# A new order of steps on every engine, and of the loads, in a fused attention and feed-forward kernel

## Chip, cores, metric

One core of one Trainium2 chip. The metric is device microseconds (us) of that core for one execution; lower is better. The rounds of experiments ran on different chips, but each round, and so each ratio, on one chip. A profile covers about 2 us less than an execution's time, since it starts with the first instruction and ends with the last.

## The reference

```python
def _attn_ref(q, k, v):                       # B, H, S, D = 8, 8, 576, 64
    chunk = 64
    ...
    scores = (1/sqrt(D)) * q_c @ k_c.T        # within each chunk of 64 tokens
    attn = softmax(scores)
    out = attn @ v_c

def _moe_ref(x, w1, w2, w3, w_out):           # x: 4608 x 512, d_ff 1024
    a = x @ w1
    b = x @ w2
    h = a * b @ w3
    return h @ w_out
# x of the second part is the first part's output, heads side by side; float32 in and out
```

## The kernel before

The kernel is written as small steps, and a string gives the order in which they are emitted. Every instruction goes through a helper, `inorder`, that holds it to the order of emission, so the string fixes the order on each engine, the order of the loads and which waits exist. The 18 blocks of 256 tokens are numbered 0 to 17.

```python
ORDER = """
R0 R1 v0 q1 i0 k1 v1 i1 i2 q2 k2 v2 i3 q3 k3 v3 q4 k4 v4 o h0 h1 D0.0.16.64 K0 T0.0 K1 T0.1 q5 k5 v5
S0 T1.0 E0 P0 D0.1.4.512 T1.1 q6 k6 v6 N0.0 S1 D1.0.5.512 X0.0 N0.1 X0.1 A0.0 E1 B0.0 C0.0 P1 M0.0
...
"""
    for step in ORDER.split():
        do[step[0]](*(int(n) for n in step[1:].split(".") if n))
```

| letters | engine | what |
|---|---|---|
| q k v i o h | DMA, issued by GpSimd | loads; `i` brings a quarter of w1 and w2 |
| T, G | VectorE, DMA | transpose of q or k to qkT; for blocks 8 and up, moves between partitions to qkm |
| S, E, P | TensorE, ScalarE, TensorE | scores, exp, attention times v |
| N, X, H | VectorE, VectorE, DMA | normalise, transpose to xt (to xm from block 8 on, then moves xm to xt) |
| A, B | TensorE | one group of x @ w1 and x @ w2, in the two halves of one PSUM tile |
| C, M | ScalarE, VectorE | copy of A's half to a_sb; product of a_sb and B's half |
| V W Z | VectorE, TensorE, ScalarE | w3 @ w_out, once |
| O, Y, Q | TensorE, ScalarE, DMA | output matmul, copy to o_sb, store |
| D | TensorE | dummy matmuls on zeros |

```python
    ps = ctx.enter_context(tc.tile_pool(name="ps", bufs=4, space=bass.MemoryType.PSUM))
    def psum(name):
        return ps.tile([P, 2, 512], f32, tag="p", name=name)     # two halves of 512
    ...
    def do_AB(p, j, f, which):                                   # which: 0 is A, 1 is B
        ...
                mm(ps_t[p, j][:, which, i * n:(i + 1) * n],
                   lhsT=(w1, w2)[which][:, ki, f * P:(f + 1) * P], rhs=rhs[:, ki],
                   start=(ki == 0), stop=(ki == KO - 1))
    def do_C(p, j):
        a_t[p, j] = msb.tile([P, 512], f32, tag="a_sb", bufs=3, name="a_sb")
        inorder(nc.scalar.copy(a_t[p, j][:], ps_t[p, j][:, 0, :]))
    def do_M(p, j):
        ...
        inorder(nc.vector.tensor_mul(o, view(a_t.pop((p, j))[:]), view(ps_t.pop((p, j))[:, 1, :])))
```

The softmax here doesn't subtract the row's maximum and nothing guards it: scores larger than these inputs give would overflow.

## Time and profile before

| | before |
|---|---|
| time, median of 4 executions beside the new kernel | 245.07 us (244.9 to 246.0) |
| TensorE busy in the profile | 226.6 us, 93% of the span |
| VectorE, ScalarE busy | 63%, 35% |

TensorE is the bound, so a wait of TensorE is what an order can win or lose. The waits of TensorE by releaser, kernel before (columns: engine, what it wrote and line, then what ended the wait; us in total, times, longest):

```profile
PE z_ps L92 <- DVE qkT L188: 8.1, 2, 7.3
...
PE s_ps L92 <- DMA qkm<-qkT: 1.0, 1, 1.0
PE s_ps L92 <- issue: 0.8, 2, 0.5
PE ab_ps L92 <- DVE xt L263: 0.6, 2, 0.3
```

The first line is the start, when nothing is loaded yet. The others are what an order can still win after it: S12 waiting for moves, holes inside S3 and S7 for which the profile knows no releaser ("issue"), and two waits for xt.

### The profile page before, as it was taken

To read this page: it belongs to the slowest core of one execution; us is meant where nothing else is said; L and a number is where in the kernel's file an instruction comes from. 1 tells how busy PE (TensorE), PEld (TensorE's weight loads), DVE (VectorE), ACT (ScalarE), POOL (GpSimd) and SP (SyncE) were. 2 spreads that over 40 slices of the span, in tenths; PEclk is the share of its full clock that TensorE was granted. 3 is DMA by queue.
4 is the path that set the end of the run, shared out by engine and by line. 5 is a ranking of instruction groups with operands and counts; after the bars stand their busy time and mean duration, and the time that the engine had idled before them with its cause. 6 is when DMAs were issued, how large, how long until landed. Compare 5 with 4: busy or idle time off the path is not lost.

```text
span 244.5 us, 6344 instructions
## 1 busy us (share of the span) xinstructions
PE 226.6 (93%) x2731; PEld 120.8 (49%) x2753; DVE 154.2 (63%) x232; ACT 85.2 (35%) x116; POOL 82.9 (34%) x110
## 2 busy tenths in 40 slices
PE   1279999999999999999998999999999999999994
PEld 1238777874445444444444444444444444444443
DVE  1675899698799588999997789918530232143000
ACT  2411423423233344425234335253231433332322
POOL 8847875556994346763740000000000000000000
PEclk9999999999999999999999999999999999999999
DMA  7999999999999999999999913735502200400244
GB/s 178 181 183 179 185 168 203 197 192 168 166 174 217 223 222 262 180 214 197 200 210 247 294 42 89 173 78 208 149 0 88 86 0 0 173 1 1 86 172 172
DMA packets 93595, 37.63 MB, mean 154 GB/s; under 512 B 75008, under 2 KB 86528, under 8 KB 93568
## 3 DMA queue, kind: packets, MB, share of 16 engines
q0 software_dynamic: 82592, 18.88, 83.1%
q1 hardware_dynamic: 9936, 17.83, 24.1%
q10 hardware_dynamic: 1040, 0.52, 0.8%
q8 instruction: 21, 0.34, 0.6%
q14 instruction: 6, 0.05, 0.1%
HBM read 38.80 MB, written 9.44 MB: 197 GB/s over the span
## 4 chain that ended last, share of the span: by engine, by line
PE 78%; DMA 8%; DVE 6%; SPq 3%; issue 2%; POOL 2%; ACT 1%; DVEq 0%; POOLq 0%
PE ab_ps L92 43%; PE o_ps L92 22%; PE w_ps L92 6%; DMA qkm<-qkT 5%; DMA qk<-in_k_dram 3%; PE s_ps L92 3%; SPq L180 3%; PE pv L92 2%; PE z_ps L92 2%; DVE qkT L188 2%; DVE xt L263 1%; DVE xn L251 1%; DVE ab L332 1%; POOL vbuf L95 1%; ACT a_sb L317 1%
## 5 line engine op out<-in xcount | busy, mean ns | idle before, releaser
L92 PE MATMUL ab_ps<-xt,w 128*128 128x512 bf16 (+1 forms) x681 | 126.8, 342 | 1.1 <-DVE xt L263 0.6
L92 PEld LDWEIGHTS <-w 128*128 128x128 bf16 x704 | 67.4, 98 | 55.2 <-DVE xt L263 1.2
L332 DVE TENSOR_TENSOR ab<-a_sb,ab_ps 128x512 bf16<-128x512 f32 x71 | 47.9, 676 | 45.0 <-ACT a_sb L317 44.9
L317 ACT COPY a_sb<-ab_ps 128x512 f32<-128x512 f32 x71 | 41.6, 586 | 81.0 <-PE ab_ps L92 79.1
L92 PE MATMUL o_ps<-w3o,ab 128*128 128x512 bf16 (+1 forms) x285 | 63.3, 373 | 0.6
L188 DVE STREAM_TRANSPOSE qkT<-qk 128x1024 bf16<-128x1024 bf16 x36 | 45.1, 1289 | 9.2 <-ACT qk L139 5.5
L92 PEld LDWEIGHTS <-ab 128*128 128x128 bf16 x296 | 28.5, 98 | 32.3
L95 POOL DMA_DIRECT2D vbuf<-in_v_dram x40 | 33.9, 856 | 20.9 <-DMA qk<-in_q_dram 6.4
L362 ACT COPY o_sb<-o_ps 128x1024 f32<-128x1024 f32 x17 | 17.2, 1012 | 44.8 <-PE o_ps L92 41.3
L251 DVE TENSOR_TENSOR xn<-pv,rc 128x512 bf16<-128x512 f32 x36 | 24.9, 691 | 1.2
L95 POOL DMA_DIRECT2D qk<-in_k_dram x23 | 18.0, 784 | 9.1 <-DMA vbuf<-in_v_dram 6.2
L95 POOL DMA_DIRECT2D qk<-in_q_dram x23 | 18.2, 793 | 6.9 <-DMA qk<-in_k_dram 1.5
L221 ACT ACTIVATE e<-s_ps 128x1024 bf16<-128x1024 f32 x16 | 15.9, 1026 | 3.4 <-PE s_ps L92 3.3
L92 PE MATMUL w_ps<-wo,w3T 128*128 128x512 bf16 x62 | 13.9, 379 | 0.1
L271 DVE STREAM_TRANSPOSE xm<-xn 128x512 bf16<-128x512 bf16 x20 | 13.6, 697 | 0.2
L248 DVE RECIPROCAL rc<-pv 128x8 f32<-128x8 f32 x36 | 6.9, 191 | 10.5 <-PE pv L92 10.5
L95 POOL DMA_DIRECT2D w<-in_moe_w_dram x16 | 11.1, 697 | 4.5 <-DMA wo<-in_moe_w_out_dram 1.5
L92 PEld LDWEIGHTS <-e 64*32 64x32 bf16 (+1 forms) x832 | 7.9, 97 | 7.9 <-issue 6.1
L263 DVE STREAM_TRANSPOSE xt<-xn 128x512 bf16<-128x512 bf16 x16 | 11.4, 711 | 0.5
L92 PEld LDWEIGHTS <-qkT 32*64 32x64 bf16 x512 | 5.7, 117 | 11.3 <-DVE qkT L188 9.6
L92 PE MATMUL pv<-vbuf,e 64*32 64x65 bf16 (+1 forms) x832 | 10.1, 198 | 1.1 <-ACT e L221 1.1
L355 DVE COPY o_sb<-o_ps 128x256 f32<-128x256 f32 x1 | 0.4, 425 | 16.0 <-PE o_ps L92 16.0
(23 smaller groups left out, 53.9 us busy)
## 6 DMA issues: line engine op xcount, KB each, us to landing
out_dram<-o_sb SPq DMA_DIRECT2D x17, 512.0 KB, 3.5
qkm<-qkT SPq DMA_DIRECT2D x40, 128.0 KB, 6.3
vbuf<-in_v_dram POOLq DMA_DIRECT2D x32, 128.0 KB, 8.7
w<-in_moe_w_dram POOLq DMA_DIRECT2D x16, 256.0 KB, 9.6
qk<-in_q_dram POOLq DMA_DIRECT2D x11, 256.0 KB, 7.6
qk<-in_k_dram POOLq DMA_DIRECT2D x11, 256.0 KB, 9.2
xt<-xm SPq DMA_DIRECT2D x40, 64.0 KB, 2.9
wo<-in_moe_w_out_dram POOLq DMA_DIRECT2D x4, 256.0 KB, 6.9
```

The source lines that it names most:

```text
L92: return inorder(nc.tensor.matmul(*a, **kw))
L95: return inorder(nc.gpsimd.dma_start(dst, src))
L180: inorder(nc.sync.dma_start(dst, src))
L188: inorder(nc.vector.transpose(qkT_t[g][:, :, p % 2, s, heads(h)].rearrange("p e h (y t) -> p h t e y", t=2), qk_t[p][:, s, heads(h)].rearr ...
L221: inorder(nc.scalar.activation(e_t[p][:, :, heads(hh)], s_t[p][:].rearrange("p u (h q) -> p u h q", q=CH)[:, :, heads(hh)], Exp, scale=sca ...
L248: inorder(nc.vector.reciprocal(rc[:], pv[:, :, :, D:W]))
L251: inorder(nc.vector.tensor_mul(xn_t[p][:, u], pv[:, :, :, 0:D], rc.to_broadcast([P, 2, 4, D])))
L263: inorder(nc.vector.transpose(new_xt(g)[:].rearrange("p (o t) -> p o t", o=KO)[:, :, t0:t0 + UT] .rearrange("p o (m y) -> p m o y", y=BL), ...
L271: inorder(nc.vector.transpose(xm_t[g][:, u, :, m].rearrange("p o (c y) -> p c o y", y=BL), xn_t[p][:].rearrange("p u r m d -> p (u r) m d" ...
L317: inorder(nc.scalar.copy(a_t[p, j][:], ps_t[p, j][:, 0, :]))
L332: inorder(nc.vector.tensor_mul(o, view(a_t.pop((p, j))[:]), view(ps_t.pop((p, j))[:, 1, :])))
L362: inorder(nc.scalar.copy(o_sb[:], ps_t.pop(p)[:]))
```

## The change

By its author's account, the order was searched for anew by simulated annealing, on a cost model that had been refitted to instruction fetch, to the moves between partitions and to early landings of loads. Apart from the order, and the dummies (D) that may now write other tiles, nothing changes: no computation is added or taken away. The diff, cut:

```diff
-R0 R1 v0 q1 i0 k1 v1 i1 i2 q2 k2 v2 i3 q3 k3 v3 q4 k4 v4 o h0 h1 D0.0.16.64 K0 T0.0 K1 T0.1 q5 k5 v5
-S0 T1.0 E0 P0 D0.1.4.512 T1.1 q6 k6 v6 N0.0 S1 D1.0.5.512 X0.0 N0.1 X0.1 A0.0 E1 B0.0 C0.0 P1 M0.0
-A0.1 N1.0 X1.0 B0.1 C0.1 N1.1 A0.2 X1.1 B0.2 C0.2 M0.1 A1.0 T2.0 B1.0 C1.0 M0.2 A1.1 T2.1 q7 k7 v7
...
+R0 R1 v0 q1 k1 v1 i0 i2 i1 q2 k2 i3 v2 q3 k3 v3 q4 k4 h0 o h1 v4 D0.0.0.16.64 K0 T0.0 K1 T0.1 q5 k5
+v5 D0.0.0.8.512 S0 T1.0 E0 T1.1 q6 k6 P0 v6 S1 N0.0 E1 N0.1 X0.0 X0.1 A0.0 B0.0 C0.0 P1 M0.0 A0.2
+N1.0 B0.2 N1.1 A0.1 X1.0 X1.1 C0.1 B0.1 C0.2 A1.0 T2.0 B1.0 C1.0 A1.1 M0.1 M0.2 B1.1 C1.1 T2.1 q7 k7
...
+B6.1 G5.1 C6.1 X8.0 A6.4 M6.1 P9 v15 q16 k16 C6.4 B6.4 N9.0 A6.2 M6.4 B6.2 X8.1 C6.2 N9.1 A6.5 X9.0
...
+B6.7 T12.1 O4 E11 T13.0 C6.7 M6.7 T13.1 P10 v16 q17 k17 Y4 A8.3 G6.0 N10.0 B8.3 N10.1 C8.3 A8.0 M8.3
...
+A14.5 M12.7 C12.3 A12.0 B12.3 A12.4 M12.3 B12.4 X16.1 C12.4 X17.0 C12.0 A12.6 C14.5 M12.4 H8.0 B14.5
+C12.6 B12.0 M14.5 B12.6 M12.0 Q11 A12.5 X17.1 M12.6 B12.5 H8.1 A14.7 A14.6 C14.7 C12.5 B14.6 C14.6
...
-    def do_D(which, p, n, cols):
-        d, key = (s_t, p) if which == 0 else (ps_t, (p, 0))
+    def do_D(which, p, j, n, cols):
+        d, key = ((s_t, p), (ps_t, (p, j)), (pv_t, (p, 0)))[which]
```

A step of TensorE can thus be followed by a step of another group, and C can stand ahead of its own B (`C0.1 B0.1`, `C6.4 B6.4`, `C14.5 ... B14.5`).

More of the change, by code (lines that the diff above doesn't have):

```diff
@@ L9 @@
 ORDER = """
-R0 R1 v0 q1 i0 k1 v1 i1 i2 q2 k2 v2 i3 q3 k3 v3 q4 k4 v4 o h0 h1 D0.0.16.64 K0 T0.0 K1 T0.1 q5 k5 v5
-S0 T1.0 E0 P0 D0.1.4.512 T1.1 q6 k6 v6 N0.0 S1 D1.0.5.512 X0.0 N0.1 X0.1 A0.0 E1 B0.0 C0.0 P1 M0.0
-A0.1 N1.0 X1.0 B0.1 C0.1 N1.1 A0.2 X1.1 B0.2 C0.2 M0.1 A1.0 T2.0 B1.0 C1.0 M0.2 A1.1 T2.1 q7 k7 v7
-B1.1 C1.1 M1.0 S2 M1.1 A0.3 E2 T3.0 B0.3 C0.3 P2 M0.3 A1.2 N2.0 X2.0 B1.2 C1.2 N2.1 A1.3 X2.1 B1.3
-C1.3 M1.2 A2.0 T3.1 q8 k8 v8 B2.0 C2.0 M1.3 S3 T4.0 A2.1 E3 M2.0 B2.1 T4.1 q9 k9 C2.1 P3 v9 M2.1
@@ L15 @@
-A2.2 N3.0 B2.2 C2.2 X3.0 A2.3 N3.1 B2.3 X3.1 C2.3 M2.2 S4 M2.3 A3.0 E4 B3.0 C3.0 A3.1 M3.0 B3.1 C3.1
-V0 A3.2 M3.1 B3.2 C3.2 V1 A3.3 M3.2 B3.3 C3.3 V2 W0 M3.3 V3 W1 Z0 V4 V5 W2 Z1 V6 V7 T5.0 Z2 W3 T5.1
-q10 k10 T6.0 T6.1 P4 v10 q11 k11 Z3 S5 N4.0 O0 E5 X4.0 N4.1 X4.1 T7.0 O1 T7.1 Y0 Q0 T8.0 P5 v11 q12
-k12 Y1 S6 T8.1 O2 Q1 E6 N5.0 X5.0 N5.1 X5.1 O3 T9.0 T9.1 Y2 G4.0 P6 v12 q13 k13 A4.0 N6.0 B4.0 G4.1
-Y3 X6.0 N6.1 C4.0 A4.1 X6.1 B4.1 C4.1 M4.0 Q2 S7 Q3 M4.1 A4.2 E7 T10.0 B4.2 C4.2 T10.1 P7 v13 q14
@@ L20 @@
-k14 A4.3 M4.2 B4.3 N7.0 C4.3 A4.4 X7.0 M4.3 B4.4 C4.4 N7.1 A4.5 M4.4 B4.5 C4.5 X7.1 S8 M4.5 S9 E8
-A4.6 T11.0 B4.6 E9 T11.1 P8 v14 q15 k15 C4.6 A4.7 M4.6 G5.0 B4.7 C4.7 N8.0 A6.0 M4.7 B6.0 N8.1 C6.0
-G5.1 A6.1 X8.0 B6.1 M6.0 C6.1 X8.1 P9 v15 q16 k16 A6.2 M6.1 N9.0 B6.2 C6.2 N9.1 A6.3 M6.2 B6.3 C6.3
-X9.0 A6.4 M6.3 B6.4 C6.4 X9.1 A6.5 T12.0 H4.0 B6.5 C6.5 M6.4 A6.6 M6.5 B6.6 T12.1 H4.1 C6.6 S10 S11
-M6.6 E10 A6.7 T13.0 B6.7 E11 P10 v16 q17 k17 T13.1 C6.7 O4 M6.7 G6.0 N10.0 N10.1 X10.0 G6.1 P11 v17
@@ L25 @@
-Y4 X10.1 O5 N11.0 N11.1 Q4 X11.0 X11.1 T14.0 A8.0 H5.0 Y5 B8.0 T14.1 C8.0 A8.1 M8.0 B8.1 H5.1 C8.1
-T15.0 A8.2 B8.2 M8.1 C8.2 T15.1 Q5 A8.3 B8.3 C8.3 M8.2 G7.0 S12 M8.3 S13 E12 A8.4 T16.0 B8.4 E13
-G7.1 P12 T16.1 C8.4 A8.5 B8.5 M8.4 C8.5 N12.0 A8.6 M8.5 B8.6 C8.6 N12.1 A8.7 M8.6 B8.7 C8.7 X12.0
-P13 M8.7 A10.0 X12.1 B10.0 C10.0 N13.0 A10.1 M10.0 B10.1 N13.1 C10.1 A10.2 X13.0 B10.2 M10.1 C10.2
-X13.1 S14 S15 M10.2 E14 A10.3 H6.0 T17.0 B10.3 E15 P14 T17.1 C10.3 A10.4 H6.1 M10.3 B10.4 C10.4
-N14.0 A10.5 M10.4 B10.5 G8.0 C10.5 N14.1 A10.6 M10.5 B10.6 C10.6 X14.0 P15 G8.1 X14.1 A10.7 M10.6
@@ L31 @@
-B10.7 N15.0 C10.7 O6 N15.1 M10.7 X15.0 X15.1 H7.0 S16 Y6 S17 O7 E16 E17 H7.1 P16 Y7 O8 Q6 N16.0 Q7
-N16.1 X16.0 X16.1 P17 Y8 A12.0 N17.0 Q8 B12.0 N17.1 C12.0 A12.1 X17.0 B12.1 M12.0 C12.1 X17.1 A12.2
-M12.1 H8.0 B12.2 C12.2 A12.3 M12.2 B12.3 C12.3 H8.1 A12.4 M12.3 B12.4 C12.4 A12.5 M12.4 B12.5 C12.5
-A12.6 M12.5 B12.6 C12.6 A12.7 M12.6 B12.7 C12.7 O9 M12.7 O10 Y9 Q9 A14.0 Y10 B14.0 C14.0 Q10 A14.1
-M14.0 B14.1 C14.1 A14.2 M14.1 B14.2 C14.2 A14.3 M14.2 B14.3 C14.3 A14.4 M14.3 B14.4 C14.4 A14.5
-M14.4 B14.5 C14.5 A14.6 M14.5 B14.6 C14.6 A14.7 M14.6 B14.7 C14.7 O11 M14.7 O12 Y11 Q11 A16.0 Y12
@@ L37 @@
-B16.0 C16.0 Q12 A16.1 M16.0 B16.1 C16.1 A16.2 M16.1 B16.2 C16.2 A16.3 M16.2 B16.3 C16.3 A16.4 M16.3
-B16.4 C16.4 A16.5 M16.4 B16.5 C16.5 A16.6 M16.5 B16.6 C16.6 A16.7 M16.6 B16.7 C16.7 O13 M16.7 O14
-Y13 Q13 O15 Y14 Q14 O16 Y15 Q15 Y16 Q16 O17
+R0 R1 v0 q1 k1 v1 i0 i2 i1 q2 k2 i3 v2 q3 k3 v3 q4 k4 h0 o h1 v4 D0.0.0.16.64 K0 T0.0 K1 T0.1 q5 k5
+v5 D0.0.0.8.512 S0 T1.0 E0 T1.1 q6 k6 P0 v6 S1 N0.0 E1 N0.1 X0.0 X0.1 A0.0 B0.0 C0.0 P1 M0.0 A0.2
+N1.0 B0.2 N1.1 A0.1 X1.0 X1.1 C0.1 B0.1 C0.2 A1.0 T2.0 B1.0 C1.0 A1.1 M0.1 M0.2 B1.1 C1.1 T2.1 q7 k7
@@ new lines @@
+v7 A0.3 M1.1 S2 C0.3 M1.0 B0.3 E2 M0.3 P2 A1.2 T3.0 B1.2 N2.0 A1.3 N2.1 B1.3 C1.3 X2.0 C1.2 X2.1
+T3.1 q8 k8 v8 A2.0 M1.2 C2.0 S3 T4.0 B2.0 E3 A2.1 M1.3 B2.1 M2.0 C2.1 T4.1 q9 k9 P3 v9 A2.2 M2.1
+B2.2 N3.0 A2.3 X3.0 N3.1 S4 C2.3 C2.2 X3.1 B2.3 E4 M2.2 A3.3 M2.3 B3.3 V0 A3.2 V1 B3.2 C3.2 V2 C3.3
+A3.1 W0 V3 M3.3 M3.2 A3.0 V4 B3.1 C3.0 V5 Z0 B3.0 W1 C3.1 M3.1 T5.0 W2 V6 Z1 V7 T5.1 q10 k10 W3 Z2
+M3.0 T6.0 T6.1 S5 Z3 P4 v10 q11 k11 E5 O0 N4.0 T7.0 T7.1 N4.1 O1 Y0 X4.0 Q0 T8.0 T8.1 P5 v11 q12 k12
+Y1 X4.1 O2 N5.0 Q1 T9.0 N5.1 S6 T9.1 O3 E6 X5.0 G4.0 Y2 X5.1 G4.1 P6 v12 q13 k13 A4.0 Y3 N6.0 B4.0
@@ new lines @@
+X6.0 C4.0 Q2 A4.1 N6.1 B4.1 M4.0 C4.1 X6.1 S7 M4.1 A4.2 E7 T10.0 B4.2 C4.2 T10.1 P7 v13 q14 k14 A4.3
+M4.2 N7.0 B4.3 C4.3 A4.4 M4.3 A4.5 N7.1 C4.4 B4.4 X7.0 C4.5 S8 M4.4 S9 E8 B4.5 T11.0 A4.6 E9 M4.5
+B4.6 C4.6 X7.1 P8 v14 q15 k15 M4.6 A4.7 T11.1 B4.7 C4.7 N8.0 A6.0 G5.0 B6.0 M4.7 C6.0 N8.1 A6.1 M6.0
+B6.1 G5.1 C6.1 X8.0 A6.4 M6.1 P9 v15 q16 k16 C6.4 B6.4 N9.0 A6.2 M6.4 B6.2 X8.1 C6.2 N9.1 A6.5 X9.0
+B6.5 M6.2 H4.0 A6.3 X9.1 B6.3 C6.3 C6.5 A6.6 M6.3 H4.1 B6.6 M6.5 C6.6 T12.0 A6.7 S10 M6.6 S11 Q3 E10
@@ new lines @@
+B6.7 T12.1 O4 E11 T13.0 C6.7 M6.7 T13.1 P10 v16 q17 k17 Y4 A8.3 G6.0 N10.0 B8.3 N10.1 C8.3 A8.0 M8.3
+G6.1 B8.0 T14.0 C8.0 P11 v17 A8.2 M8.0 X10.0 B8.2 C8.2 N11.0 O5 X10.1 N11.1 M8.2 X11.0 A8.1 X11.1
+H5.0 Y5 T14.1 A8.5 C8.1 A8.4 T15.0 B8.5 H5.1 C8.4 C8.5 B8.1 A8.6 M8.1 B8.4 M8.5 C8.6 S12 M8.4 S13
+E12 B8.6 T15.1 A8.7 E13 M8.6 G7.0 B8.7 C8.7 P12 M8.7 A10.3 N12.0 B10.3 Q4 C10.3 G7.1 A10.0 M10.3
+A10.1 N12.1 C10.0 B10.0 C10.1 Q5 P13 M10.0 B10.1 N13.0 A10.6 M10.1 B10.6 C10.6 N13.1 A10.2 X12.0 S14
@@ new lines @@
+M10.6 C10.2 S15 B10.2 E14 T16.0 O6 E15 M10.2 T16.1 T17.0 A10.5 T17.1 Y6 P14 B10.5 C10.5 G8.0 O7
+M10.5 N14.0 N14.1 Q6 G8.1 X12.1 X13.0 P15 Y7 A10.4 N15.0 B10.4 Q7 N15.1 C10.4 O8 X13.1 M10.4 X14.0
+X14.1 S16 Y8 S17 A10.7 E16 Q8 B10.7 H6.0 C10.7 O9 E17 M10.7 X15.0 H6.1 O10 Y9 Q9 H7.0 P16 Y10 A12.2
+N16.0 B12.2 X15.1 C12.2 O11 N16.1 H7.1 M12.2 Q10 P17 Y11 A12.7 N17.0 B12.7 X16.0 C12.7 A12.3 N17.1
+A14.5 M12.7 C12.3 A12.0 B12.3 A12.4 M12.3 B12.4 X16.1 C12.4 X17.0 C12.0 A12.6 C14.5 M12.4 H8.0 B14.5
@@ new lines @@
+C12.6 B12.0 M14.5 B12.6 M12.0 Q11 A12.5 X17.1 M12.6 B12.5 H8.1 A14.7 A14.6 C14.7 C12.5 B14.6 C14.6
+M12.5 B14.7 M14.6 A14.1 M14.7 A14.3 A16.1 C14.3 B14.1 C16.1 C14.1 B16.1 M14.1 B14.3 A16.3 M14.3
+B16.3 C16.3 A12.1 M16.3 A14.0 M16.1 B12.1 C14.0 C12.1 A16.6 M12.1 A14.4 B14.0 C14.4 A16.5 M14.0
+B14.4 C16.6 B16.6 O12 M16.6 B16.5 Y12 O13 C16.5 Q12 M16.5 M14.4 A14.2 Y13 A16.2 C14.2 Q13 B16.2
+C16.2 B14.2 A16.7 M14.2 A16.4 C16.7 B16.4 B16.7 O14 M16.7 M16.2 A16.0 B16.0 C16.0 C16.4 O15 Y14
+M16.4 M16.0 Q14 O16 Y15 Q15 Y16 Q16 O17
```

## The prediction

> **What bounds the kernel now.** I read the page first, then the windows of 10 us, then the chain, then the time line around every place where TensorE did not advance.
>
> ```profile
> PE 226.6 (93%) x2731; PEld 120.8 (49%) x2753; DVE 154.2 (63%) x232; ACT 85.2 (35%) x116; POOL 82.9 (34%) x110
> PE   1279999999999999999998999999999999999994
> DVE  1675899698799588999997789918530232143000
> DMA  7999999999999999999999913735502200400244
> ```
>
> TensorE is full from about 20 us to the end, so it is the bound; but the DMA engines are as full until 138 us (slice 23), and VectorE has slices at 9 until 150 us. Reordering changes no engine's total, so what it can win is the time in which TensorE stands or runs slowly. To size that I took the steady pace from the chain:
>
> ```profile
> 182.72 6.64 PE o_ps L92 x30
> 189.36 13.81 PE ab_ps L92 x64
> ```
>
> 64 matmuls of 512 columns take 13.81 us, 216 ns each. So an A or B step of a late group is 0.86 us, an O or W step (16 matmuls) 3.45, and an A or B step of an early group (8 matmuls of 256 columns) 0.87 by its spacing in the time line. S and P take 0.64 and 0.63 us for the first eight tiles, 0.32 and 0.38 for the other ten, and each switch from the big matmuls to the small ones costs about 0.11 more. Laid end to end, all A, B, S, P, W and O give 218.1 us, plus 26 switches x 0.11 = 2.9: 221.0. The first real matmul starts at 9.54 and the last ends at 241.2, which is 231.7. **The loss is thus about 10.7 us**, and the change can win no more than part of that. It lies here:
>
> ```profile
> 9.54 1.07 PE L92 MATMUL z_ps<-qkT 32*64 32x64 bf16 x64 [7.32 <-DVE qkT L188]
> 11.74 0.75 PE L92 MATMUL pv<-vbuf,e 64*32 64x65 bf16 x64 [1.13 <-ACT e L221]
> 12.83 1.49 PE L92 MATMUL z_ps<-zero 128*128 128x512 bf16 x3 [0.33 <-issue]
> 16.91 1.49 PE L92 MATMUL z_ps<-zero 128*128 128x512 bf16 x3 [0.22 <-issue]
> 18.19 2.28 PE L92 MATMUL z_ps<-xt,w 128*128 128x256 bf16 x16
> ```
> ```profile
> 88.26 0.31 PE L92 MATMUL s_ps<-qkT 32*64 32x64 bf16 x13 [0.50 <-issue]
> 132.00 0.93 PE L92 MATMUL s_ps<-qkm 64*64 64x64 bf16 x63 [1.03 <-DMA qkm<-qkT]
> 35.73 1.92 PE L92 MATMUL ab_ps<-xt,w 128*128 128x256 bf16 x16 [0.32 <-DVE xt L263]
> ```
>
> Some 7 us are lost before 21 us (idle, and matmuls on zeros that only keep TensorE busy). Later: two waits for xt (at 25.0 and 35.7, some 0.5 each), a hole inside S3 (0.5) and one inside S7 (0.7), and S12, which takes 1.71 us instead of 0.25, so 1.5. After 142 us nothing is lost.
>
> [...]one instruction queue moved 21 packets, 0.34 MB, 16 KB each, and the holes inside S3 and S7 are 765 weight loads apart[...].[...] moves between partitions took up to 9.7 us to land while loads ran, 2.3 at best.[...] The zeros at 12.8 to 18.2 us step by 0.42 us, twice 216 ns, and the clock record at 1.0 starts at 18.9 us[...].
>
> **The change, part by part.** It removes and adds no computation; 9 dummy matmuls of 512 columns, in two places, become 8 in one, all ahead of S0.
>
> (a) **Loads at the start.** k1 goes ahead of w1/w2 quarter 0.
>
> ```profile
> 13.72 1.31 DVE L188 STREAM_TRANSPOSE qkT<-qk 128x1024 bf16<-128x1024 bf16 x1 [2.84 <-DMA qk<-in_k_dram]
> 30.42 1.32 DVE L188 STREAM_TRANSPOSE qkT<-qk 128x1024 bf16<-128x1024 bf16 x1 [0.39 <-DMA qk<-in_q_dram]
> ```
>
> The first line is T1.1, waiting for k1. Landings of loads follow one another at 1.3 to 1.5 us for 256 KB. Two of them in front go, so k1 lands at 13.7 - 2.7 = 11.0, and T1.1 ends at 12.3 instead of 15.0. N0 and X0 for both halves took 3.2 us after it (14.93 to 18.14), so A0.0 can start near 15.8 instead of 18.1, with its weights landing at 14 to 15.4. This would be 2.3 us, or about 1 if TensorE is then still at half clock.
> But the second line says that it does not last. T3.0 waits for q3, and what is loaded up to q3 is the same set in both orders, so q3 lands at 30.4 again. After the change T3.0 stands ahead of N2 and X2 on VectorE: 30.4 + 1.3 + N2.0, N2.1, X2.0, X2.1 (2 x 0.91 + 2 x 0.71) = 34.95. Before, one M (0.7) came between, and X2.1 ended at 35.67. A2.0 waits for X2.1 in both. **So the start is worth 0.7 us, not 2.3.** From T3.0 on VectorE works without pause to X3.1 (at about 44.6 instead of 45.1), which again gives A3 some 0.7 us earlier. The hole in S3 is inside this figure.
>
> (b) **S7** keeps P6, A4.0, B4.0, A4.1, B4.1 ahead of it[...]. I expect its hole of 0.5 to 0.7 again. No gain.
>
> (c) **S12** waited for the last move of qkm, landed at 131.86.
>
> ```profile
> 122.80 9.06 DMA qkm<-qkT
> ```
>
> The transposes that feed these moves stand 0.7 us later on VectorE, but S12 now has 4.3 us more TensorE work ahead of it (114.2 instead of 109.9, counted in the two orders). Without that wait S12 would start near 130.8 before, so near 134 to 135 after: the wait goes. **-1.5 us.** A small hole at P13 (0.13) goes too: -0.1.
>
> (d) **One switch more** to small matmuls (27 instead of 26): +0.1.
>
> (e) **A8 comes early.**
>
> ```profile
> 108.75 5.65 SPq L180 DMA_DIRECT2D xt<-xm  x8
> ```
>
> Those are H4's eight moves; the last landed at 120.67, over 6 us after its issue. A8.0 ran at 123.5, without waiting. In the new order the first A8 step has 3.9 us less TensorE work ahead of it, so it is due at about 119.2, while X9.1, which feeds the last moves, has the same VectorE work ahead of it, and the moves still queue behind G5's eight. If they land at 120.5 to 121.2 TensorE waits 1.3 to 2. The author says that moves were fitted anew, so perhaps they land sooner. I put +0.9, the middle of 0 and 1.8.
>
> (f) **A and B of one tile drawn apart** (32 tiles), with C between them in 26. In the trace C starts only after B's end, though it reads A's half; dependencies seem to go by tile. C ahead of B lets M follow B at once, and in all but one of the 26 another TensorE step covers C (0.59 us). The exception, B0.1, waits for its weights anyway. Counting the four PSUM tiles round, the tightest reuses have 0.0 to 0.3 us of room: I allow +0.2 for small waits. Tail: O15, O16, O17 close it as before, no change.
>
> Sum: -0.7 - 1.5 - 0.1 + 0.1 + 0.9 + 0.2 = -1.1; 244.96 - 1.1 = 243.9. I shade to **243.7**, since an order searched for on a fitted model has more likely avoided (e) than hit it.
>
> **Rivals.** (1) *The early start survives.* If q3 lands earlier because the queue of loads packs better, the 2.3 us stay: about 241.5 to 242. For it: T1.1's 2.84 us wait is real and goes. Against: the DMA engines are at 9 in slices 1 to 22, so the stream has no slack to give. (2) *The new order loses to moves and PSUM*: A8 waits 2 us, S10 (before, its moves landed 0.6 us ahead of it) waits too, tiles turn late; 245 to 246. For it: moves of 6 to 9 us during the loads, VectorE at 9 there. Against: the search weighed it. (3) *Half clock.* The dummies now end near 5.7 us[...]; 16 matmuls of 256 columns at 0.21 instead of 0.11 cost 1.7 us. Against its mattering: q3 holds A2.0 back anyway, with room of about 1.5 us. If both bind, 244.5.
>
> **Range and chances.** 2% is 4.9 us, that is 240.06; it takes nearly half of all loss, and the start, two thirds of it, is held by the loads. Rival 1 with nothing lost in (e) gives 241.5, rival 2 up to 246. Runs of the kernel before spread over 1.1 us. So 241.7 to 245.4 at 8 in 10; faster by over 2% 0.04, slower by over 2% 0.02.
>
> **What would show it.** (a) k1 landing near 11, A0.0 near 16, and A2.0 near 35.0 with a wait for xt of over 1 us, T3.0 again waiting for q at about 30.4. If A2.0 starts before 34, the step "q3 lands at the same time" is wrong. (b) A hole of 0.5 us with releaser "issue" in S7. (c) No wait for qkm at S12. (e) A wait of TensorE for DMA xt<-xm near 119; its absence would give 0.9 us back. (f) No rows of TensorE waiting for ACT a_sb. After about 160 us no wait of TensorE above 0.3 us; one there would make the prediction wrong on the high side.

For (f), the profile before has C0.0 starting 0.03 us after B0.0's last matmul (20.48 and 20.51).

## The result

| | before | after |
|---|---|---|
| median of 4 executions | 245.07 us | 247.77 us |
| range | 244.9 to 246.0 | 247.45 to 247.97 |
| ratio, 95% interval | | 1.0101 (1.0072 to 1.0130) |

Ratios in this document are the mean time of one kernel's runs over the mean of the other's in the same rounds, so they are not quite the ratio of the medians quoted. Executions over 1.5% slower than the fastest of the same kernel are left out of the means. All outputs are right. A later repeat (e15 below) gave 1.0076. The new order is slower, by 1.9 to 2.5 us; the prediction said 1.3 faster, and its range ended at 245.4.

The page of the kernel after: busy time, and TensorE and DMA in 40 slices.

```profile
PE 228.4 (93%) x2731; PEld 121.5 (50%) x2752; DVE 152.4 (62%) x232; ACT 83.3 (34%) x116; POOL 82.9 (34%) x110
PE   7268989999999989999899999999998999999994
DMA  7999999999999999999999480554531500022044
```

The 7 in the first slice is the dummies. Before, TensorE had one slice of 8 between slice 3 and the last, at 21, which is S12. Now it has 9 there and five 8s, counted from 0: at 3, 5, 14, 19 and 30, that is at 18, 31, 86, 117 and 184 us. What stands there, the waits of TensorE, kernel after, say:

```profile
PE ab_ps L92 <- DVE xt L263: 2.5, 2, 1.9
PE ab_ps L92 <- ACT a_sb L317: 1.8, 3, 0.8
...
PE ab_ps L92 <- DMA xt<-xm: 0.8, 1, 0.8
PE s_ps L92 <- issue: 0.7, 1, 0.7
```

The wait for qkm is gone, as meant. New are three waits for ScalarE's copies, 1.8 us, and one for the moves to xt, 0.8. (Of the 2.5 us for xt, 1.9 come before A0.0, where the kernel before ran dummies and work at half clock: its zeros of 512 columns step by 0.42 us there, and matmuls of that width by 0.216 us later.) The time line of TensorE has the first of the three, kernel after:

```profile
19.46 3.29 PE L92 MATMUL ab_ps<-xt,w 128*128 128x256 bf16 x24
23.42 5.40 PE L92 MATMUL ab_ps<-xt,w 128*128 128x256 bf16 x48 [0.67 <-ACT a_sb L317]
...
35.46 1.05 PE L92 MATMUL ab_ps<-xt,w 128*128 128x256 bf16 x8 [0.56 <-DVE xt L263]
```

The second row starts with B0.1. It follows A0.1 directly, with C0.1 emitted between. ScalarE's time line shows the copy that it waited for:

```profile
22.79 1.08 ACT L317 COPY a_sb<-ab_ps 128x512 f32<-128x512 f32 x2 [3.33 <-PE ab_ps L92]
```

C0.1 starts as A0.1 ends and takes 0.59 us, and B0.1 starts at its end. C reads one half of the tile and B writes the other, yet B waits, 0.67 us. Two stretches of VectorE's time line, kernel after, show what this did to block 3:

```profile
30.64 0.69 DVE L332 TENSOR_TENSOR ab<-a_sb,ab_ps 128x512 bf16<-128x512 f32 x1 [0.75 <-ACT e L221]
31.25 1.31 DVE L188 STREAM_TRANSPOSE qkT<-qk 128x1024 bf16<-128x1024 bf16 x1
```

The second row is T3.0. It doesn't wait for q3 (landed at 30.36): it waits its turn behind M0.3, the first row. The row names an exp that ended at 30.55, but M0.3 doesn't read that. It reads the copy of A0.3, which was done at 29.45, and B0.3, whose last matmul ended at 30.53. So it waits for B0.3, that is for TensorE, which is late.

Three rows of TensorE's time line much later, kernel after: B6.4, A8.3 and B14.5.

```profile
105.82 2.53 PE L92 MATMUL ab_ps<-xt,w 128*128 128x512 bf16 x10 [0.30 <-ACT a_sb L317]
...
120.86 3.61 PE L92 MATMUL ab_ps<-xt,w 128*128 128x512 bf16 x16 [0.75 <-DMA xt<-xm]
...
189.20 5.12 PE L92 MATMUL ab_ps<-xt,w 128*128 128x512 bf16 x23 [0.79 <-ACT a_sb L317]
```

And ScalarE's row of the same place as the last, kernel after:

```profile
187.59 2.05 ACT L317 COPY a_sb<-ab_ps 128x512 f32<-128x512 f32 x4 [3.73 <-PE ab_ps L92]
```

These four copies are C12.4, C12.0, C14.5 and C12.6, in that order. Five TensorE steps stand between A14.5 and B14.5, but the copy stands third in ScalarE's queue, behind C12.4, and C12.4 is emitted behind B12.4 and waits for its end. So C14.5 ran at 188.54 to 189.15, and B14.5 after it.

Step starts (the start of a step's first weight load), in us from each span's start, show where the two kernels drift apart ("before" is the faster of its two profiles, e1; e16 and e18 are told below):

| step | before (e1) | after | e16 | e18 |
|---|---|---|---|---|
| A0.0 | 17.69 | 15.23 | 15.24 | 15.42 |
| A1.0 | 24.68 | 24.19 | 22.92 | 23.31 |
| A2.0 | 35.62 | 35.46 | 34.47 | 34.85 |
| O0 | 67.00 | 67.15 | 66.16 | 66.54 |
| S7 | 86.50 | 86.78 | 85.81 | 86.05 |
| O17 | 236.56 | 238.19 | 238.40 | 235.02 |

2.5 us are won at A0.0, and at O0 nothing is left. The rest is lost behind S7.

### The profile page after: what moved, and what is told of

Same layout as the page of the kernel before. It is cut to its first block, busy times and chain, and to the rows that moved or that the text cites. A ratio compares the mean times of both kernels' runs of the same rounds, so it can differ in the third digit from the quotient of the medians.

```text
span 245.3 us, 6362 instructions
## 1 busy us (share of the span) xinstructions
PE 228.4 (93%) x2731; PEld 121.5 (50%) x2752; DVE 152.4 (62%) x232; ACT 83.3 (34%) x116; POOL 82.9 (34%) x110
## 4 chain that ended last, share of the span: by engine, by line
PE 57%; DMA 25%; DVE 5%; POOL 5%; issue 3%; SPq 2%; ACT 1%; POOLq 0%; DVEq 0%
PE ab_ps L92 36%; PE o_ps L92 18%; DMA qk<-in_k_dram 10%; DMA qk<-in_q_dram 9%; DMA qkm<-qkT 3%; POOL vbuf L95 3%; DMA xt<-xm 3%; DVE qkT L188 2%; POOL qk L95 2%; SPq L180 2%; PE pv L92 2%; PE s_ps L92 1%; ACT a_sb L317 1%; DVE xn L251 1%; DVE ab L332 1%
## 5 line engine op out<-in xcount | busy, mean ns | idle before, releaser
L92 PE MATMUL ab_ps<-xt,w 128*128 128x512 bf16 (+1 forms) x697 | 132.0, 344 | 5.8 <-DVE xt L263 2.5
L188 DVE STREAM_TRANSPOSE qkT<-qk 128x1024 bf16<-128x1024 bf16 x36 | 45.8, 1296 | 5.9 <-ACT qk L139 5.3
L221 ACT ACTIVATE e<-s_ps 128x1024 bf16<-128x1024 f32 x17 | 17.0, 1026 | 9.2 <-PE s_ps L92 9.1
L263 DVE STREAM_TRANSPOSE xt<-xn 128x512 bf16<-128x512 bf16 x16 | 10.7, 688 | 0.1
L373 DVE STREAM_TRANSPOSE w3T<-w 128x1024 bf16<-128x1024 bf16 x8 | 9.4, 1217 | 1.1 <-DVE ab L332 0.9
L92 PEld LDWEIGHTS <-w3T 128*128 128x128 bf16 x64 | 6.3, 98 | 7.1
```

Source lines behind the costliest of these rows:

```text
L92: return inorder(nc.tensor.matmul(*a, **kw))
L188: inorder(nc.vector.transpose(qkT_t[g][:, :, p % 2, s, heads(h)].rearrange("p e h (y t) -> p h t e y", t=2), qk_t[p][:, s, heads(h)].rearr ...
L221: inorder(nc.scalar.activation(e_t[p][:, :, heads(hh)], s_t[p][:].rearrange("p u (h q) -> p u h q", q=CH)[:, :, heads(hh)], Exp, scale=sca ...
L263: inorder(nc.vector.transpose(new_xt(g)[:].rearrange("p (o t) -> p o t", o=KO)[:, :, t0:t0 + UT] .rearrange("p o (m y) -> p m o y", y=BL), ...
L373: inorder(nc.vector.transpose(w3T_t[f][:].rearrange("p k (f y) -> p f k y", y=BL), w3[:, NB * f:NB * (f + 1), :].rearrange("p f (k x) -> p ...
```

## The experiments

Eighteen runs were made, two of them repeats (e1, e15). Theory at first: the loss is the copies placed ahead of their own B, plus the early A8. Rivals: it is the half clock at the start; it is the holes named "issue"; it is the waits for moves alone.

### Which part loses: e1 to e4

e1 is the kernel before, unchanged, to see what repeats give.

> The kernel before, unchanged, to see how a run and its profile differ from one another. Its first profile came from an execution of 246.56 us while its other runs took 244.9 to 246.0; the profiles of before and after differ by 0.8 us of span, the times by 2.6. Theory A (the loss is in the late part: one wait for moves at A8.3, one at B14.5): the ratio is 1.000, and a second profile has the same start (first real matmul group A0.0 at 17.8 us, A1.0 at 25.0). Theory B (the start of the two kernels differs more than the profiles show[...]): the second profile has an earlier A1.0 or end, by some 1.5 us.

Ratio 1.0021 (0.999 to 1.0051). So intervals of about 0.3% are what six runs give, and single profiles differ by up to 2.4 us in span (242.5 to 244.9).

```diff
 e2_late_only:  ORDER = before up to T6.1, then new from there
 e3_early_only: ORDER = new up to T6.1, then before from there
 e4_to_k17:     ORDER = new up to k17 (past block 6's last M), then before from G6.0
```

> The order of before up to T6.1 (the end of W3), the new order from there. Theory A: the loss is in this part, so ratio to before about 1.010 to 1.013 (the new start had gained 0.5 us, which is missing here). Theory B: 1.000 to 1.004.

> The new order up to T6.1 with its new loads and dummies, the order of before from there. Theory A: 0.5 us faster than before, ratio 0.998. Theory B: the start loses, ratio 1.005 to 1.010.

> The new order up to the last load (M6.7, k17), the order of before from there: no A8 steps ahead of P11 and O5, no mixed tail. Theory A: about as fast as before, ratio 0.998 to 1.001, as the new order led by 0.1 to 0.2 us at this point in the profiles. Theory B: 1.005 to 1.010, as in the early part alone.

e2: 1.0141 (1.0101 to 1.0181). e3: 1.0003 (0.9974 to 1.0032). e4: 1.0094 (1.0053 to 1.0135). **The whole loss is in the late part, and the early part, where the prediction had its gain, gains nothing.** e2's profile has the waits of the new kernel in the same three places. Measured by how late the step starts against the steady pace, they are B6.4 0.35, A8.3 0.68 and B14.5 0.95 (new kernel, measured so: 0.37, 0.79 and 0.95; the waits view gives somewhat less for both). e4 missed its expectation, and its profile shows why it tells little: the seam made waits of its own (P11 0.59 and A12.1 0.45 for copies to o_sb, S12 1.33 for moves), so it doesn't say how the loss divides at that point.

### The copies: e7, e16

```diff
 e7_after_c_moved (new order)
-C6.4 B6.4
+B6.4 C6.4
-A12.6 C14.5 M12.4 H8.0 B14.5 C12.6 B12.0
+A12.6 M12.4 H8.0 C12.6 B14.5 C14.5 B12.0
 e16_after_c_three: the same, and
-C0.1 B0.1 C0.2
+B0.1 C0.1 C0.2
```

> The kernel after with two copies moved: C6.4 behind B6.4, and C14.5 behind B14.5 with C12.6 ahead of it. In the profile of after B6.4 stood 0.35 us and B14.5 0.95 us, the latter for a copy of ScalarE. If B waits for C because both use one tile: both waits go, nothing takes their place, span -1.3 us against after, so ratio to before about 1.005 where after has 1.010. Rival: the waits are for VectorE freeing tiles, and they move to the next step: 1.009 to 1.010.

> The kernel after with three copies moved: C6.4, C14.5 and C12.6 as in e7 (1.0037), and C0.1 behind B0.1. In the profile of after TensorE waited three times for a copy of ScalarE, 1.8 us in all; e7 took two of them away and 0.7 us was left, at B0.1. If that is the same dependency by tile: no wait of TensorE for ACT a_sb is left, A1.0 starts 0.6 to 0.8 us earlier than in after (24.0 to 24.2), and as little as 0.2 to 0.5 of it reaches A2.0 (T3.0 can't start before q3 at 30.4); ratio 1.002 to 1.004. Rival (B0.1 waits for its weights, which land at 22.3): A1.0 as in after, ratio 1.0037.

e7: 1.0037 (1.0009 to 1.0065), and only the 0.7 us of B0.1 are left of the waits for a_sb. e16: 1.0011 (0.9971 to 1.0052), and none is left. The new kernel itself gave 1.0101 and 1.0076 in its two tries. So moving three copies (which at B14.5 also puts C12.6 ahead of C14.5), with nothing else changed, gives back 0.65 to 0.9%, 1.6 to 2.2 us, which fits the 1.8 us of the waits view. The two sides did not run in the same rounds: each ratio is against the kernel before in its own, so the difference is uncertain by about 0.5%. No run tried the two halves as tiles of their own. TensorE's time line of e7 runs through at B14.5, without the wait:

```profile
185.84 8.37 PE L92 MATMUL ab_ps<-xt,w 128*128 128x512 bf16 x38
```

**The copies ahead of their B are the loss, to within these intervals.** The wait for moves at A8.3 (0.75) comes on top; S12, which costs less than before, pays for it.

e16 also shows what was hidden behind B0.1. VectorE's time line, e16:

```profile
30.24 1.32 DVE L188 STREAM_TRANSPOSE qkT<-qk 128x1024 bf16<-128x1024 bf16 x1 [0.28 <-DMA qk<-in_q_dram]
```

T3.0 now does wait for q3, and TensorE's time line of e16 has A2.0 at 34.47, where the prediction had put it at 35.0:

```profile
19.19 8.28 PE L92 MATMUL ab_ps<-xt,w 128*128 128x256 bf16 x72
...
34.47 1.05 PE L92 MATMUL ab_ps<-xt,w 128*128 128x256 bf16 x8 [0.92 <-DVE xt L263]
...
120.43 5.30 PE L92 MATMUL ab_ps<-xt,w 128*128 128x512 bf16 x16 [2.04 <-DMA out_dram<-o_sb]
```

The first row runs through where the new kernel has its hole of 0.67. The last is A8.3 and the next three steps. TensorE now came to A8.3 1.7 us earlier than in the new kernel (P10 at 117.95 and not 119.66), and waited 2.04 us in place of 0.75. The releaser named is the one that came last by the profile; in the new kernel, e7, e15 and e16 alike A8.3 starts 0.46 us after the last of H4's moves has landed (119.97 in e16, 120.40 in the new kernel), so it is the moves. And the row has 16 matmuls in 5.30 us; 3.61 is usual (row 120.86 above). Windows of TensorE, e16 (columns: us, PE busy, granted clock, DMA share, GB/s):

```profile
122.00:124.00 2.00, 2.00 (x6) 0.50 1.73 263
124.00:126.00 2.00, 2.00 (x40) 0.98 1.55 191
```

The clock was at half (0.50) from 120.67 for 3.41 us. The wait cost its own 2 us, and the half clock behind it 1.7 us more. The new kernel's window has 1.00 there, behind its wait of 0.75. The half clock behind the wait was seen in this one profile; that the wait brought it on is not shown. Of e16's six executions, three had a mean granted clock of 0.97 (247.64, 247.50 and 245.83 us) and three 0.98 or 1.0 (244.91 to 246.17), but only one was profiled, and e18 below, the fastest kernel, has 0.97 to 0.98 in five of six, so these means don't tell it either. In the profiled execution (247.64 us) wait and half clock ate the whole gain (last matmul at 242.25, and at 242.04 in the new kernel); over the six the gain stands.

### A8 and its moves: e9, e17

```diff
 e9_after_c_o5 (e7) and e17_c_three_o5 (e16): the output step O5 ahead of A8.3
-Y4 A8.3 ... N11.0 O5 X10.1 ... H5.0 Y5 T14.1
+Y4 O5 A8.3 ... C8.3 Y5 ... N11.0 X10.1 ... H5.0 T14.1
```

> The kernel after with the two copies moved as in the run before (that alone gave 1.0037), and O5 taken from behind B8.2 to ahead of A8.3, so that A8.3 has 3.45 us more TensorE work ahead of it. In after A8.3 stood 0.8 us; the last move it needs landed at 120.4. If that landing is what it waits for: the wait goes and none replaces it, ratio about 1.000. Rival (VectorE is behind there, and the wait moves to S12, P11 or P12): ratio 1.003 to 1.004.

> The same with O5 ahead of A8.3 as in e9 (1.0033). If the causes named so far are all: what is left of the new order against before are waits of 0.2 to 0.6 at A8.5 and S12 that e9 showed; ratio 1.001 to 1.003. Rival (something that the profiles do not show costs the new order more): 1.004 or above.

e9: 1.0033 (1.0004 to 1.0062), beside e7's 1.0037. e17: 0.9989 (0.9956 to 1.0021), beside e16's 1.0011. The wait at A8.3 is gone in both, the mean granted clock in e17's profile was 1.000 (e16's 0.972), but smaller waits come instead: in both, A8.4 waits 0.39 for xn, and S12 takes some 0.6 longer than its work, 0.2 of it a wait for ab. The gain is within the intervals. The wait for H4 was real, but not removed by this: part of it moved on to the next steps. H4's moves landed 5.9 to 7.1 us after issue in the profiles of the new kernel, e7, e15 and e16; moves to xt from 187 us on, in the new kernel's profile, took 1.9 to 2.0.

### S12 and its moves: e5

```diff
 e5_before_s12_later (order before): S12 and S13 two A/B steps later
-S12 M8.3 S13 E12 A8.4 T16.0 B8.4 E13 G7.1 P12 T16.1 C8.4 A8.5 B8.5 M8.4 C8.5 N12.0 A8.6 M8.5 B8.6 C8.6
+M8.3 A8.4 T16.0 B8.4 C8.4 S12 S13 E12 T16.1 M8.4 A8.5 G7.1 E13 B8.5 C8.5 P12 A8.6 M8.5 N12.0 B8.6 C8.6
```

> The kernel before with S12 and S13 two A/B steps (1.73 us of TensorE work) later, nothing else: part (c) of the change alone. Its wait for the moves of qkm was 1.2 to 1.4 us in three profiles. If the wait is a matter of S12's place alone: the wait goes, no other wait of TensorE takes its place, span -1.2 us, ratio 0.995. Rival: the moves and VectorE are the limit there and the wait reappears at P12, P13 or A10.0: ratio 0.999 to 1.001.

0.9981 (0.9957 to 1.0005). S12 runs through; TensorE's time line, e5:

```profile
132.66 0.71 PE L92 MATMUL s_ps<-qkm 64*64 64x64 bf16 x64
```

So the wait at S12 can be removed alone, in a few words. What that is worth is less clear: of the 1.5 us, 0.5 are seen in the time, and the interval just includes no gain. Waits of 0.2 to 0.6 (S10, P12, P13) stand in that profile.

### The holes named "issue": e6, e11, e12, e13, e14

```diff
 e6_before_s7_later, e11_before_s7_b (order before): S7 behind two more A/B steps
-S7 Q3 M4.1 A4.2 E7 T10.0 B4.2 C4.2 T10.1 P7 v13 q14 k14 A4.3 M4.2 B4.3 N7.0 C4.3 A4.4 X7.0 M4.3 B4.4
+Q3 M4.1 A4.2 T10.0 B4.2 C4.2 S7 T10.1 M4.2 A4.3 E7 B4.3 C4.3 P7 v13 q14 k14 N7.0 A4.4 M4.3 X7.0 B4.4     (e6)
+Q3 M4.1 A4.2 B4.2 C4.2 S7 M4.2 T10.0 T10.1 A4.3 E7 B4.3 C4.3 P7 v13 q14 k14 M4.3 A4.4 N7.0 X7.0 B4.4     (e11)
 e12_before_both: e11 and e5 together
 e13_before_spread: P5 O2 S6 A4.0 B4.0 P6 O3 A4.1 B4.1 S7 on TensorE (small and big work mixed);
 e14_spread_s12: e13 and e5 together
```

What the expectations call late instruction fetch is the theory of these holes: that TensorE stands until a packet of the queue that the page calls "instruction" has landed.

> The kernel before with S7 one A/B pair later and P7 one pair later, nothing else. S7 [...] had a hole of 0.7 us in each profile of before, 0.9 of after. If it is instruction fetch that comes late[...]: 1.73 us more work ahead of the hole fills it, the hole shrinks to under 0.1, ratio 0.997. Rival (the hole belongs to the matmuls of S7, its weights or its PSUM): it moves with S7 and keeps 0.7 us, ratio 1.000.

> S7 of the kernel before one A/B pair later, again. The first try lost its gain to a wait of 0.7 us at A4.4 for M4.2, which that edit had put behind two transposes; here M4.2 goes ahead of them, and M4.3 ahead of N7. If the hole is late instruction fetch: no hole in S7, no wait at A4.4, ratio 0.997. Rival as before: 1.000.

> The kernel before with S12 later (0.9981 alone) and S7 later as in the run above, to see whether the two add up: 0.995 to 0.996 if so. Rival: what is won at S7 is lost again at S10, whose moves land at a time of their own (0.1 to 0.6 us of wait in several profiles): 0.998.

> The kernel before with P5, O2, S6, A4.0, B4.0, P6, O3, A4.1, B4.1, S7 in this order instead of P5, S6, O2, O3, P6, A4.0, B4.0, A4.1, B4.1, S7: the same steps, the small ones spread so that each block of 127.5 load-matmul pairs lasts at least 6.3 us by TensorE's own work (before: 8.2, then 4.6). In all profiles holes with releaser issue stand at pairs 223, 479, 607, 734, 1371, 1499, whatever step is there, and a block came 5.3 to 7 us after the one before it was begun. If that pace is the cause: no hole in S7 and none at pair 1499, no new wait, ratio 0.997. Rival (moving steps only moves the loss, as with S7 alone): 1.000.

> The same with S12 and S13 two steps later (0.9981 alone). If the holes are settled by spacing: about 0.994 to 0.996, faster than both kernels. Rival (S10 is then due before the moves of G5 land, wait up to 0.7 us): 0.998.

Ratios: e6 1.0010 (0.9985 to 1.0035), e11 1.0005 (0.9971 to 1.0038), e12 1.0005 (0.9971 to 1.0039), e13 0.9989 (0.996 to 1.0018), e14 1.0009 (0.998 to 1.0038). None gains. In e6 the hole of S7 went, but A4.4 then waited 0.71 for M4.2, which I had left behind two transposes: the edit's fault. In e11 that was mended, and the hole turned up 128 load-matmul pairs further on (pair 1499, not 1371). TensorE's time line, e11 and then e14:

```profile
95.58 0.57 PE L92 MATMUL s_ps<-qkm 64*64 64x64 bf16 x48 [0.35 <-issue]
```
```profile
87.92 0.31 PE L92 MATMUL s_ps<-qkT 32*64 32x64 bf16 x13 [0.72 <-issue]
```

Over all profiles, the holes named "issue" of more than 0.24 us (those in front of dummies left out) lie at the load-matmul pairs 223, 479, 607, 734, 1371 and 1499, whatever step stands there: the distance is a multiple of 127.5 pairs to within about one, and such a stretch is called a block here. In the profiles of both kernels the instruction queue moved 21 packets of 16 KB, for 2752 and 2753 weight loads, so some 131 pairs a packet: that a packet belongs to a block is an estimate from these numbers. Each hole ends 1.3 to 1.8 us after a packet of that queue has landed (before: packet 85.73 to 86.75, S7 goes on at 88.26). At these holes, the packet had landed 3.0 to 5.8 us after the block ahead of it was begun, and that block lasted 4.5 to 7.4 us. Where the packet landed after 1.1 to 3.1 us, blocks of 4.1 to 4.7 us ran without a hole. So in these profiles TensorE stands where a packet comes late and the 127.5 pairs ahead are work of less time (S and P are 64 pairs in 0.64 us). e14 had the block stretched to 6.3 us and still waited 0.72; there the packet landed at 86.32, 5.6 us after the block was begun at 80.72. That the packet is what TensorE waits for is inferred from the places and the times; no run removed the late packet itself. After 135 us no wait named "issue" in the profiles of the two kernels is above 0.2 us.

e13, whose ratio of 0.9989 fits its expectation of 0.997 as well as no gain, did what it was meant to in its profile: the hole of S7 is gone (0.13 left) and S12's wait, which the edit doesn't touch, nearly so (0.17). But that execution had also started 1.0 us later than e1's (O0 at 68.00 and not 67.00), so the profile doesn't show what this is worth. No order of these runs brought a clear gain by removing these holes.

### The half clock at the start: e8, e10

Half clock at the start is read from two things: the zeros of 512 columns step by 0.42 us (12.8 to 18.2 us, kernel before), twice the later 216 ns, and the record of the granted clock at 1.0 begins at 18.94 us before and 20.52 after.

```diff
 e8_after_warm (new order)
-v5 D0.0.0.8.512 S0 T1.0 E0 T1.1 q6 k6 P0 v6 S1 N0.0
+v5 D0.0.0.26.512 S0 T1.0 E0 T1.1 D2.0.0.4.512 q6 k6 P0 v6 S1 D1.0.0.9.512 N0.0
 e10_after_d_moved (new order)
-v5 D0.0.0.8.512 S0 ... S1 N0.0
+v5 S0 ... S1 D1.0.0.5.512 N0.0
```

> The kernel after with more dummy matmuls: 26 instead of 8 ahead of S0, 4 between S0 and P0, 9 between S1 and A0.0, so that TensorE is busy from 2 us on[...]. In after its clock fell to half at 7.8 us (where it had risen at all) and rose for good at 20.5. Theory that the loads hold the start: A0.0 to B0.1 run at full clock and P1 ends about 1.5 us earlier, but A2.0 still waits for q3 and starts at 34.9 to 35.1 instead of 35.46; ratio to before 1.008 (after has 1.010). Rival (the half clock is what lost the early gain): A2.0 starts at 34 or earlier, ratio 1.003 to 1.005.

> The kernel after with its 8 dummies of 512 columns taken from ahead of S0 and 5 put between S1 and A0.0, where TensorE waits 2 us for xt anyway. The number of TensorE instructions ahead of A0.0 falls by 6[...]. If the half clock costs the start: the clock rises between 15 and 18.5 us instead of at 20.5, P1 ends 0.7 to 1.5 us earlier; A2.0 then starts 0.3 to 0.5 us earlier (q3 lands at 30.4, and 34.95 is the earliest that this allows); ratio 1.008 against 1.010. Rival (the start is slow for another cause): A0.0 and B0.0 take 3.5 us as in after, ratio 1.010.

e8: 1.0173 (1.0148 to 1.0197), the slowest of all. e10: 1.0071 (1.0046 to 1.0096), within its interval what the new order gives. In e8 the clock stood at full from 5.7 to 15.9 us. In its TensorE time line:

```profile
16.20 0.43 PE L92 MATMUL s_ps<-qkT 32*64 32x64 bf16 x15 [3.37 <-issue]
```

With the added dummies ahead, S1 stood 3.4 us at pair 223, holes of 1.3 us (A2.2) and 0.5 us (A4.4) followed, and all was lost again; why the hole at 223 was so long is not shown. (The fall of the clock at 7.8 us, of which e8's expectation speaks, is in e4's profile; the new kernel's own shows no early rise.) In e10 the clock is up at 16.5 us, 4 us before the new order's 20.5. Two rows of TensorE's time line, e10:

```profile
18.26 0.82 PE L92 MATMUL z_ps<-xt,w 128*128 128x256 bf16 x6 [1.02 <-issue]
...
31.08 0.28 PE L92 MATMUL pv<-vbuf,e 64*32 64x65 bf16 x23 [0.30 <-issue]
```

Again A2.0 starts only at 35.14. The clock rose 4 us earlier, and A2.0 came only 0.3 us earlier; at O0 e10 was at 67.86, behind the new order's 67.15. **The half clock at the start is not the loss.**

### A repeat, and the best of both: e15, e18

e15 is the new order, unchanged.

> The kernel after, unchanged, beside the same runs of before: 1.010 as the first time if the verdict is stable; its profile shows the waits at A8.3 (0.8), B6.4 (0.35), B14.5 (0.95) again, as those come from its order, and holes at pair 1371 of varying length (0.6 to 1.3).

1.0076 (1.0046 to 1.0106), with the same waits: a_sb 1.8 us in three places, A8.3 0.9.

```diff
 e18_early_s12: ORDER = new up to T6.1, then before from there, with
-C0.1 B0.1 C0.2
+B0.1 C0.1 C0.2
 and S12 and S13 two A/B steps later, as in e5
```

> The new order up to T6.1 with C0.1 behind B0.1, then the order of before with S12 two steps later: what each part gave at best. The new start was level with before (1.0003), S12 alone 0.9981. If the wait at B0.1 was what held the start: 0.995 to 0.997. Rival ([...]the loads hold the start at about the same A3 time whatever its first steps do): 0.998 to 0.999.

**0.9933 (0.9903 to 0.9962)**, median 244.22 us (243.92 to 244.54) beside 245.9: faster than both kernels, and more than was expected. The waits of TensorE, e18, whole:

```profile
PE z_ps L92 <- DVE qkT L188: 4.0, 1, 4.0
PE ab_ps L92 <- DVE xt L263: 2.8, 2, 1.9
PE z_ps L92 <- DVE zero L109: 1.2, 1, 1.2
PE pv L92 <- ACT e L221: 1.1, 1, 1.1
PE ab_ps L92 <- DMA out_dram<-o_sb: 0.2, 1, 0.2
```

Behind A2.0 only 0.2 us of waiting are left. Beside e3 (1.0003), which is the same order but for B0.1 and S12, and e5 (0.9981), which has S12's part alone, it suggests that the early start, without B0.1's wait, is worth something to the end (the intervals of e18 and e5 just touch). Here the first A8 step stands behind O5, as before, so the moves of H4 had landed when it came, and the time won could be kept. One more thing differs: e18's profile has no hole in S7, where e1's has one of 0.76 us. Of its lead of 1.5 us over e1 at O17, 0.5 are the early start, 1.3 S12 and 0.65 the missing hole, less about 0.9 of small waits. Whether the hole went because of the order or by chance, no run tells.

## Why the prediction was wrong

It was wrong in sign: 1.3 us faster predicted, 1.9 to 2.5 slower measured. By its own steps:

- **(a) Loads at the start, -0.7: about 0.** k1 landed at 10.84 (said: 11.0), A0.0 started at 15.23 (said: 15.8, though its own sum, 12.3 and 3.2, gives 15.5), q3 landed at 30.36 (30.4). But TensorE came to B0.3 late, so M0.3 and not q3 held T3.0, and A2.0 was at 35.46 (35.0), 0.2 to 0.3 ahead of the kernel before; at O0 nothing was left. The reason is B0.1's 0.67 us, a part of (f). With that wait removed (e16) T3.0 waited for q3 and A2.0 came at 34.47: the mechanism was right and was undone by another step.
- **(b) S7, 0: right.** Its hole was 0.7 to 0.9.
- **(c) S12, -1.5 and P13 -0.1: right for S12.** It took 0.25 us and not 1.71. The small hole went to P12 (0.23) rather than away.
- **(d) One switch, +0.1: right.**
- **(e) A8, +0.9: right**, 0.75 in the waits, and H4's last move landed at 120.40, where it had said 120.5 to 121.2. But this is the size with TensorE late. With TensorE on time the wait is 2.0 (e16): rival 2's size.
- **(f) A and B drawn apart, +0.2: this step failed.** It measured 1.8 us in three waits. "In all but one of the 26 another TensorE step covers C" was checked by looking for a step between A and B. That is not enough. B6.4 had such a step, P9, but it takes 0.38 us and the copy 0.59. B14.5 had enough work between, but its copy stood in ScalarE's queue behind a copy that waited for a later B. And the one exception, B0.1, was waved off with "waits for its weights anyway": they had landed at 22.27, before A0.1 ended. The prediction named the sign that would prove it wrong on this point, rows of TensorE waiting for ACT a_sb, and there are three.

The sum, against the profile e1 (last matmul at 240.41, after 242.04, so +1.6): (a) 0.85 more than said, (f) without B0.1 1.1 more (B6.4 0.35 and B14.5 0.95 by their late starts, less the 0.2 allowed), (c) 0.35, (b) 0.15, small holes named "issue" 0.2, (e) 0.1 less. That is 2.55 more than -1.1, or +1.45, which leaves 0.2.

Of the rivals, the second (moves and PSUM, 245 to 246) was nearest in its direction, but its mechanism held only once the copies were out of the way. The range was too narrow as well: it allowed a single term of +1.8 in (e), and none in (f).

What stays open: e17, with the three copies and A8.3 mended, is still no faster than the kernel before beyond its interval (0.9989). Against e1 its profile is 0.5 us ahead at O0 (66.48 and 67.00) and S12 costs 0.7 less (0.63 and 1.29), while A8.4, A8.1, S10, P12, P16 and the added switch give nearly all of it back: its last matmul ends at 240.27, e1's at 240.41. The order after T6.1 thus has no single cause left, only many small waits, and no run tells which of them could go. Why e18 gained 0.2 to 0.4% more than expected is not settled either; the missing hole in S7 may be part of it.

## What to carry to other kernels

When a copy is put ahead of the matmuls that fill the other half of its tile, count the time of the work between against the copy's length, and look for what stands ahead of the copy in its own engine's queue; a step "in between" proves nothing. A gain at the start lasts only if the next resource that holds (here q3, then the moves of H4) is not already the later one, so walk through the waits behind it before taking it into the sum. When a searched order loses, cut it at a seam where both orders have done the same steps, and try the halves: here the early half with one pair swapped, and one part of the late half, beat both kernels.
